# A fused attention, expert and mixing kernel: scores of odd units in other PSUM banks, half of the copies on VectorE, sums over v later

## The chip, the cores and the metric

The kernel runs on one core of one Trainium2 chip. The metric is the device time of one execution in microseconds. Before the change three runs gave 429.08, 429.33 and 431.17 us, median 429.33 us. The engines are TensorE (PE; PEld is its weight load), VectorE (DVE), ScalarE (ACT), GpSimd (POOL), and SyncE (SP), which issues the loads and stores.

## What is computed

Three parts in a row, for batch 2, sequence 768 and width 512. The change concerns the first, an attention of 8 heads with a local window and block summaries:

```
scores_l = q @ k.T / 8, kept where |i - j| < 16
k_sum, v_sum = max of k, mean of v over blocks of 32 tokens
scores_s = q @ k_sum.T / 8 + log(32)
a = softmax(concat(scores_l, scores_s))
attn = a @ concat(v, v_sum)
```

The second routes each token to one of 8 experts (two layers of 512x1024 and 1024x512, relu), the third is a trigonometric token mix with a channel mix behind it.

## The kernel before

**Units.** The attention runs over 24 units k = 3n + g. The pair n (0 to 7) is a batch and two heads, g (0 to 2) is a third of the 768 tokens. A unit has 256 queries for each of two heads, in four groups of 128 (c = 0 to 3). Each group of 64 queries sees a window of 96 keys and 24 block summaries, 120 columns in all.

**Steps of a unit.** `attn_s` (L233) computes the scores, eight matmuls of 64x120 on TensorE into the tile `sps`; units of even and odd k use different columns of the same two PSUM banks. Then VectorE adds the mask, scales and takes each row's minimum, four instructions (L249, called *mins* below), and ScalarE takes the exponential, four instructions (L251, *exps*). `attn_t` (L255) transposes the result in four matmuls on TensorE, and ScalarE copies it out of PSUM into a tile of `ptl` (L259, *copy*). `attn_v` (L261) multiplies with v into the tile `ops`, which has two PSUM banks of its own (pool `psO`). `attn_n` (L273) divides by the sum, on VectorE.

**Keys.** For each pair, `load_k` and `load_q` bring k and q in. `k_windows` (L209) spreads k into overlapping windows, on GpSimd from the second pair on. `k_max` (L220) takes the block maxima on VectorE: of the next pair's first third at g = 0, of its other two thirds at g = 1 (L223). Then GpSimd writes the summaries behind the windows (L229), and the scores of that pair can start.

**Sums over v.** `vsum(b, x)` (L176) sums blocks of v of batch b with matmuls over the third x (L181, *pv*). After the last third ScalarE copies the sums (L183), one matmul spreads them (L186, *pvb*), ScalarE copies the result into the first rows (L194) and GpSimd copies these to the other places in three instructions (L195, then twice L197). The products with v of thirds 0, 1, 2 need the first, second and third of these copies.

**Order.** The loop at L904 fixes the order on every engine: each engine runs its instructions in the order in which the program emits them. An iteration k emits the scores of unit k, the preparation of the next pair's keys, one piece of side work, the transposes and the copy of unit k-1, loads and sums over v, and products with v. Products of the first batch start at k = AV0 = 9 (up to three an iteration until they have caught up), those of the second batch at k = AV1 = 15. The table `VSUM` says in which iteration the sums over v go (first batch at k = 3, 5, 6 and the spreading at 7; second batch at 11, 11, 12 and 13). `SP` loads v of the second batch in iterations 6 and 9. When the first batch's last unit is normalized, at k = 14, the transposes for the router (`gate_T`) and then the routing (`route0`) begin. After the loop the expert weights are split and multiplied, and then the mix runs, all in a fixed order too.

Of the kernel before, what the change touches and what calls it, by code (L numbers as in the profile page):

```python
# [10 lines left out]
F32 = mybir.dt.float32  # L11
# [19 lines left out]
KC = W + NB  # L31
# [59 lines left out]
def tile_attn_moe_mix(ctx: ExitStack, tc: tile.TileContext, qT, kT, vp, gw, w1, w2, wth, wtok, wch, cst, msk, out):  # L91
    nc = tc.nc
    V, A, G, T, SP = nc.vector, nc.scalar, nc.gpsimd, nc.tensor, nc.sync

    def pool(name, bufs, stack=ctx, **kw):
        kw.setdefault("reuse_waits", "tile")
        return stack.enter_context(tc.tile_pool(name=name, bufs=bufs, **kw))
# [55 lines left out]
    psO = pool("psO", 2, sA, space=PSUM)  # L153

    sps = psS.tile([128, 2, 512], F32, name="sps")
# [7 lines left out]
    ptl = {k: pts[k] if k < NPT else spare[:, k - NPT] for k in range(NPT + NSP)}  # L163
# [7 lines left out]
    def load_v(b, g):  # L171
        SP.dma_start(vall[:, vslot(b, g)].rearrange("p c v -> p (c v)"), vp[b, g, :, 0:4 * VW])

    vps = {}

    def vsum(b, x):  # L176
        if x == 0:
            vps[b] = psM.tile([128, DM], F32, name="pv", tag="m")
        for c in range(4):
            rhs = vall[0:W, vslot(b, x), c].rearrange("p (h d) -> p h d", d=D1)[:, :, 0:D]  # L180
            T.matmul(vps[b][32 * c:32 * c + 32, :], ind[0:W, 32 * x:32 * x + 32], rhs, start=x == 0, stop=x == 2)  # L181
        if x == 2:
            A.copy(svt, vps[b])  # L183
            yield
            pb = psM.tile([128, DM], F32, name="pvb", tag="m")
            T.matmul(pb[W:KC, :], ind[:, 96:120], svt, start=True, stop=True)  # L186
            one_w = pb[W:KC, :].rearrange("p (h d) -> p h d", d=D)
            dst = [vall[W:KC, vslot(b, g)].rearrange("p c (h d) -> p c h d", d=D1)[:, :, :, 0:D] for g in range(3)]
            first = dst[0][:, 0]

            def wide(t, n):
                return t.unsqueeze(1).to_broadcast([NB, n, H, D])

            A.copy(first, one_w)  # L194
            G.tensor_copy(dst[0][:, 1:4], wide(first, 3))  # L195
            for g in (1, 2):
                G.tensor_copy(dst[g], wide(first, 4))  # L197

    def load_k(n):
        b, p = divmod(n, NP)  # L200
        kcs[n] = kp.tile([128, 800], F32, name="kc", tag="kc")
        SP.dma_start(kcs[n], kT[b, 2 * p:2 * p + 2, :, 0:800].rearrange("h d s -> (h d) s"))

    def load_q(n):
        b, p = divmod(n, NP)
        qf[n] = qp.tile([128, S], F32, name="qf", tag="qf")
        SP.dma_start(qf[n], qT[b, 2 * p:2 * p + 2].rearrange("h d s -> (h d) s"))

    def k_windows(n, lo=0, hi=NT):  # L209
        kc = kcs[n]  # L210
        if lo == 0:
            ka[n] = kp.tile([128, NT, KC], F32, name="ka", tag="ka")
        win = bass.AP(tensor=kc.tensor, offset=kc.offset + 64 * lo, ap=[list(kc.ap[0]), [64, hi - lo], [1, W]])
        dst = ka[n][:, lo:hi, 0:W]
        if n == 0:
            A.copy(dst, win)
        else:
            G.tensor_copy(dst, win)

    def k_max(n, lo, hi):  # L220
        if lo == 0:
            kss[n] = st.tile([128, NB], F32, name="ks", tag="ks", bufs=2)
        V.tensor_reduce(kss[n].rearrange("p (c x r) -> p x c r", c=4, x=3)[:, lo:hi],  # L223
                        kcs[n][:, 16 + 256 * lo:16 + 256 * hi].rearrange("p (x c r j) -> p x c r j", c=4, r=2, j=32),
                        axis=AX.X, op=ALU.max)
        if hi == 3:
            ks = kss.pop(n)
            for a_, b_ in ((0, 4), (4, NT)) if n == 0 else ((0, NT),):
                (V if n == 0 else G).tensor_copy(ka[n][:, a_:b_, W:KC], ks.unsqueeze(1).to_broadcast([128, b_ - a_, NB]))  # L229
# [1 line left out]
    kss = {}  # L231

    def attn_s(n, g):  # L233
        x = (3 * n + g) % 2
        ps = [[sps[:, h, 240 * x + 120 * a:240 * x + 120 * a + KC] for a in range(2)] for h in range(2)]
        for a in range(2):
            for r in range(2):
                for h in range(2):
                    t = 4 * g + 2 * a + r
                    hs_ = slice(64 * h, 64 * h + 64)  # L240
                    T.matmul(ps[h][a][64 * r:64 * r + 64, :], qf[n][hs_, 64 * t:64 * t + 64], ka[n][hs_, t, :],  # L241
                             start=True, stop=True)
        neg = sp.tile([128, 4, KC], F32, name="neg", tag="neg")
        mn = st.tile([128, 4], F32, name="mn", tag="mn")
        for c in range(4):
            a, h = divmod(c, 2)
            t = 2 * g + a
            v = 0 if t == 0 else (2 if t == NT // 2 - 1 else 1)
            V.tensor_tensor_reduce(out=neg[:, c, :], in0=ps[h][a], in1=mk[:, v, :], scale=-0.125, scalar=3.0e38,  # L249
                                   op0=ALU.add, op1=ALU.min, accum_out=mn[:, c:c + 1])  # L250
            A.activation(neg[:, c, :], neg[:, c, :], AF.Exp, bias=mn[:, c:c + 1], scale=-1.0)  # L251
            micro(1)
        return neg

    def attn_t(k, neg):  # L255
        tps = psT.tile([128, 4, 128], F32, name="tps", tag="t")
        for c in range(4):
            T.transpose(tps[0:KC, c, :], neg[:, c, :], idn)
        A.copy(ptl[k][0:KC], tps[0:KC])  # L259

    def attn_v(k):  # L261
        n, g = units[k]
# [597 lines left out]
    def micro(n=2):  # L860
        for _ in range(n):
            micro1()
# [7 lines left out]
    units = [(n, g) for n in range(B * NP) for g in range(3)]  # L870
    NG = len(units)
    HB = NG // 2
    AV0, AV1 = 9, 15
    VSUM = {3: [(0, 0)], 5: [(0, 1)], 6: [(0, 2)], 11: [(1, 0), (1, 1)], 12: [(1, 2)]}, (7, 13)
    spread = None
    todo, fill, norm = [], [], []
    pend, nsp, LS = None, 0, 3
# [14 lines left out]
    def finish(k, kk, ops):  # L892
        attn_n(kk, ops)
        b_, p_ = divmod(units[kk][0], NP)
        if p_ == NP - 1:
            g_ = units[kk][1]
            store_x(b_, g_)
            fill.append((k, b_, 2 * g_))
            fill.append((k, b_, 2 * g_ + 1))
            if b_ == 0 and g_ == 2:  # L900
                state["bg"] = route0()
                state["tok"], state["cool"] = "hop", 0

    for k in range(NG + 8):  # L904
        state["k"] = k
        for kk, ops in norm:
            finish(k, kk, ops)
        norm = []
        if k == AV0:
            todo.sort(key=lambda x: (units[x][1], x))  # L910
        if k < NG:
            n, g = units[k]
            cur = attn_s(n, g)
            if n + 1 < B * NP:
                if g == 0:
                    k_windows(n + 1)
                    k_max(n + 1, 0, 1)
                elif g == 1:
                    k_max(n + 1, 1, 3)
            if g == 0 and 0 < n < B * NP - 2:  # L920
                load_k(n + 2)
                load_q(n + 2)
        if 13 <= k < 19:
            SP.dma_start(yd[256 * (k - 13):256 * (k - 12), :].rearrange("(p a) (r c) -> p (a r) c", p=128, c=128),
                         zro.unsqueeze(1).to_broadcast([128, 8, 128]))
        if k == 12:
            V.tensor_copy(tri, cs[:, C_TRI:C_TRI + 128])
        side(k, False)
        if AV0 <= k < AV1 and len(todo) > 2 and todo[0] < HB:
            kk = todo.pop(0)  # L930
            finish(k, kk, attn_v(kk))
        if pend is not None:
            attn_t(k - 1, pend)
            todo.append(k - 1)
        pend = cur if k < NG else None
        for x in {6: (0, 1), 9: (2,)}.get(k, ()):
            load_v(1, x)
        if k in VSUM[1]:
            next(spread, None)
        for b_, x in VSUM[0].get(k, ()):  # L940
            spread = vsum(b_, x)
            next(spread, None)
        cnt = 0
        while todo and cnt < 2 and (k >= (AV0 if todo[0] < HB else AV1) and len(todo) > 1 or k >= NG):
            kk = todo.pop(0)
            norm.append((kk, attn_v(kk)))
            cnt += 1
        if k >= NG and nsp < LS and (0, nsp) in raws:
            split_piece(0, nsp)
            nsp += 1  # L950
        if k >= NG and not todo and not norm:
            break
        side(k, True)
# [53 lines left out]
    for n in range(8 * NL + 8):  # L1007
        j, q = divmod(n, 8)
        for half in range(2):
            h = 2 * q + half  # L1010
# [36 lines left out]
    for q in range(8):  # L1047
        n = 8 * NL + 8 + q
# [419 lines left out]
```

## Time and profile before

| | |
|---|---|
| median of 3 runs | 429.33 us |
| profiled execution | 431.33 us, span of its core 429.5 us |
| busy in the span: PE, DVE, ACT, POOL | 404.9, 305.2, 230.9, 106.4 us |
| mean granted TensorE clock | 0.987 of full speed |
| attention units 0 to 9, first to last scores | 5.53 to 24.53 us |
| last product with v | 72.7 us |
| DMA moved | 76.32 MB, mean 178 GB/s |

The profiled execution is 2.0 us above the median of the runs; 1.83 us of its time lie outside the span. Times in the rows below are microseconds from the start of the span. A matmul with fp32 operands shows as two records, so eight matmuls read x16 in a timeline.

### The profile page before, as it was taken

The numbers are of one execution on the slowest core, as the hardware profiler recorded it, in microseconds if no ns is written. First come the engines' busy times: TensorE is split into PE (matmuls) and PEld (weight loads), VectorE is DVE, ScalarE is ACT, GpSimd is POOL, SyncE is SP. The second block draws the span as 40 slices with busy tenths as digits, with TensorE's granted clock in tenths as the row PEclk, the third lists the DMA queues.
The fourth block names the chain that finished last, engine by engine and source line by source line (L and its number), as shares of the span: only waits on it lengthen the run. The fifth ranks groups of instructions, "written<-read, shape, count | busy, mean of one in ns | idle before, by whom it ended". The sixth has DMA issues, their size and how long they took to land. (4 is left out here: it accounts for less than half of the span.)

```text
span 429.5 us, 8298 instructions
## 1 busy us (share of the span) xinstructions
PE 404.9 (94%) x3109; PEld 343.1 (80%) x3109; DVE 305.2 (71%) x733; ACT 230.9 (54%) x423; POOL 106.4 (25%) x95
## 2 busy tenths in 40 slices
PE   7889998799899999999998999999999999999993
PEld 6465766598798989898987878888888788889883
DVE  5476687779797968987899588797988843622731
ACT  5875857346466667775678566564654421211300
POOL 6171703510122105040210121443334710100000
PEclk9999999899899999999999999999999999999997
DMA  8994938773787968988587352322300010100022
GB/s 301 410 389 140 338 113 275 284 277 106 263 271 246 346 225 280 335 276 310 187 300 236 127 216 99 102 75 79 119 24 8 28 39 26 49 14 27 14 75 79
DMA packets 43441, 76.32 MB, mean 178 GB/s; under 512 B 3328, under 2 KB 25088, under 8 KB 42624
## 3 DMA queue, kind: packets, MB, share of 16 engines
q1 hardware_dynamic: 41312, 68.89, 46.8%
q0 software_dynamic: 2080, 6.82, 4.3%
q8 instruction: 26, 0.43, 0.4%
q14 instruction: 23, 0.19, 0.2%
HBM read 62.85 MB, written 12.85 MB: 176 GB/s over the span
## 5 line engine op out<-in xcount | busy, mean ns | idle before, releaser
L596 DVE TENSOR_TENSOR wlo<-wraw,whi 128x1024 fp32r<-128x1024 f32 x53 | 64.4, 1219 | 13.2 <-ACT whi L595 13.2
L595 ACT CAST whi<-wraw 128x1024 fp32r<-128x1024 f32 x56 | 58.1, 1047 | 3.8 <-DMA wraw<-in_w_dram 2.7
L751 POOL DMA_INDIRECT yd<-y,ixs x13 | 16.6, 1274 | 121.8 <-ACT y L711 100.7
L251 ACT ACTIVATE neg<-neg,mn 128x120 f32<-128x120 f32 x96 | 30.3, 385 | 18.6 <-DVE mn L249 18.2
L633 PE MATMUL psh<-xl,whi 128*128 128x256 f32 x192 | 32.3, 291 | 1.9 <-DVE xl L619 1.9
L633 PE MATMUL psh<-xh,whi 128*128 128x256 f32 x192 | 32.5, 293 | 0.6 <-DVE hl L639 0.6
L633 PE MATMUL psh<-xh,wlo 128*128 128x256 f32 x192 | 31.7, 288 | 0.0
L704 PE MATMUL psy<-whi,hh 128*128 128x512 f32 x96 | 30.7, 401 | 0.0
L1203 POOL TENSOR_TENSOR r<-r,x 128x512 f32<-128x512 f32 x10 | 13.1, 1307 | 69.9 <-ACT r L1198 69.9
L704 PE MATMUL psy<-wlo,hh 128*128 128x512 f32 x96 | 29.8, 392 | 0.0
L704 PE MATMUL psy<-whi,hl 128*128 128x512 f32 x96 | 29.8, 392 | 0.0
L633 PEld LDWEIGHTS psh<-xl,whi 128*128 128x128 f32 x192 | 27.5, 198 | 2.4 <-DVE xl L619 2.4
L633 PEld LDWEIGHTS psh<-xh,whi 128*128 128x128 f32 x192 | 27.7, 199 | 1.7 <-DVE hl L639 0.8
L249 DVE CUSTOM_DVE_ANT_0 neg<-sps,mk 128x120 f32<-128x120 f32 x96 | 21.9, 278 | 9.6 <-PE sps L241 6.7
L633 PEld LDWEIGHTS psh<-xh,wlo 128*128 128x128 f32 x192 | 27.4, 198 | 0.0
L772 ACT ACTIVATE dg<-raw 128x768 f32<-128x768 f32 (+1 forms) x20 | 16.4, 818 | 18.7 <-issue 3.7
L1266 DVE SCALAR_TENSOR_TENSOR o<-psch,xTr 128x512 f32<-128x512 f32 (+1 forms) x8 | 4.4, 552 | 28.7 <-PE psch L1260 28.7
L638 ACT ACTIVATE hh<-psh 128x512 fp32r<-128x512 f32 x24 | 14.3, 595 | 17.2 <-PE psh L633 17.1
L639 DVE SCALAR_TENSOR_TENSOR hl<-psh,hh 128x512 fp32r<-128x512 f32 x24 | 16.5, 687 | 8.9 <-ACT hh L638 8.7
L704 PEld LDWEIGHTS psy<-whi,hl 128*128 128x128 f32 x96 | 18.0, 188 | 4.0
L704 PEld LDWEIGHTS psy<-wlo,hh 128*128 128x128 f32 x96 | 18.0, 188 | 3.9
L604 POOL DMA_INDIRECT xg<-xd,ixg x13 | 15.5, 1196 | 22.1 <-DVE ip L413 19.1
(456 smaller groups left out, 1122.9 us busy)
## 6 DMA issues: line engine op xcount, KB each, us to landing
wraw<-in_w_dram SPq DMA_DIRECT2D x56, 512.0 KB, 4.7
raw<-in_wtok_dram SPq DMA_DIRECT2D x12, 768.0 KB, 6.6
vall<-in_v_dram SPq DMA_DIRECT2D x6, 1040.0 KB, 9.7
kc<-in_k_dram SPq DMA_DIRECT2D x8, 400.0 KB, 6.9
qf<-in_q_dram SPq DMA_DIRECT2D x8, 384.0 KB, 7.1
xd<-xs SPq DMA_DIRECT2D x6, 512.0 KB, 5.5
yd<-zro SPq DMA_DIRECT2D x6, 512.0 KB, 6.7
x<-yd SPq DMA_DIRECT2D x12, 256.0 KB, 2.7
```

The lines of the kernel that those rows point to most:

```text
L249: V.tensor_tensor_reduce(out=neg[:, c, :], in0=ps[h][a], in1=mk[:, v, :], scale=-0.125, scalar=3.0e38, op0=ALU.add, op1=ALU.min, accum_out ...
L251: A.activation(neg[:, c, :], neg[:, c, :], AF.Exp, bias=mn[:, c:c + 1], scale=-1.0)
L595: A.copy(hi, r)
L596: (G if j == 0 and q < 3 else V).tensor_tensor(lo, r, hi.bitcast(F32), op=ALU.subtract)
L604: G.indirect_dma_start(out=t, out_offset=None, in_=xd[0:S, :] if j < 2 else xd, in_offset=bass.IndirectOffsetOnAxis(ap=ixg[:, c:c + 1], ax ...
L633: T.matmul(ps[:, mm, :], a[:, c, fs], x[:, c, :], start=n == 0, stop=n == 11)
L638: A.activation(hh, ps, AF.Relu)
L639: V.scalar_tensor_tensor(hl, ps, 0.0, hh.bitcast(F32), op0=ALU.max, op1=ALU.subtract)
L704: T.matmul(ps, a[:, f, ts_], w[:, f, :], start=q == 0 and n == 0, stop=q == 3 and n == 5)
L751: G.indirect_dma_start(out=yd, out_offset=bass.IndirectOffsetOnAxis(ap=ixs[:, c:c + 1], axis=0), in_=ysb[j, r], in_offset=None)
L772: A.activation(g, hw.bitcast(F32), AF.Copy, scale=2.0 ** -112)
L1203: eng[0].tensor_tensor(r, r, x, op=ALU.mult)
```

## The change

Four things change, all in the attention loop. (1) Units of odd k below AV0 put their scores into two tiles of the pool `psO`, the banks that the products with v use later. (2) The copy of transposed units of odd k below AV0 goes to VectorE. (3) AV0 becomes 10. (4) The table of sums over v moves back: the first batch to k = 4, 7, 8 with the spreading at 9, the second to 12, 12, 13 and 14; the spreading is now emitted right behind the scores of its iteration. The loads of v of the second batch stand in iterations 7, 8 and 10.

```diff
+    AV0, AV1 = 10, 15
...
     def attn_s(n, g):
-        x = (3 * n + g) % 2
-        ps = [[sps[:, h, 240 * x + 120 * a:240 * x + 120 * a + KC] for a in range(2)] for h in range(2)]
+        k = 3 * n + g
+        x = k % 2
+        if x and k < AV0:
+            bank = [psO.tile([128, 2, KC], F32, name=f"spo{h}", tag="o") for h in range(2)]
+            ps = [[bank[h][:, a, :] for a in range(2)] for h in range(2)]
+        else:
+            ps = [[sps[:, h, 240 * x + 120 * a:240 * x + 120 * a + KC] for a in range(2)] for h in range(2)]
...
-        A.copy(ptl[k][0:KC], tps[0:KC])
+        if k < AV0 and k % 2:
+            V.tensor_copy(ptl[k][0:KC], tps[0:KC])
+        else:
+            A.copy(ptl[k][0:KC], tps[0:KC])
...
-    AV0, AV1 = 9, 15
-    VSUM = {3: [(0, 0)], 5: [(0, 1)], 6: [(0, 2)], 11: [(1, 0), (1, 1)], 12: [(1, 2)]}, (7, 13)
+    VSUM = {4: [(0, 0)], 7: [(0, 1)], 8: [(0, 2)], 12: [(1, 0), (1, 1)], 13: [(1, 2)]}, (9, 14)
...
             cur = attn_s(n, g)
+            if k in VSUM[1]:
+                next(spread, None)
...
-        for x in {6: (0, 1), 9: (2,)}.get(k, ()):
+        for x in {7: (0,), 8: (1,), 10: (2,)}.get(k, ()):
             load_v(1, x)
-        if k in VSUM[1]:
-            next(spread, None)
```

The order of SP's instructions stays the same up to the fifth load of keys and beyond; the one difference there is that a fill of `yd` with zeros and a store of `xd` change places near k = 13. GpSimd's order doesn't change at all.

VectorE before, from the last mins of unit 6 (tile `sps`) over the maxima of the next pair's first third to the first mins of unit 7:

```order
L249 ISA neg,mn<-sps,mk 128x120
L249 ISA mn 128x1
L223 TENSOR_REDUCE ks<-kc 128x4x2
L249 ISA neg,mn<-sps,mk 128x120
L249 ISA mn 128x1
```

VectorE now, the same place (`spo` is the tile of an odd unit's scores, `pt_150` the place of unit 5 in `ptl`):

```order
L255 ISA neg,mn<-sps,mk 128x120
L255 ISA mn 128x1
L224 TENSOR_REDUCE ks<-kc 128x4x2
L266 COPY pt_150<-tps 120x512
L255 ISA neg,mn<-spo_442,mk 128x120
L255 ISA mn 128x1
L255 ISA neg,mn<-spo_443,mk 128x120
```

The copy of unit 5 stands between the maxima and the mins of unit 7; the copies of units 1, 3, 7 and 9 are placed in the same way.

TensorE before, from the scores of unit 6 to the first products with v (`pt_145` is unit 0, `pt_148` unit 3):

```order
L241 MATMUL sps<-ka,qf 64x120 x8
L258 MATMUL tps<-idn,neg 120x128 x4
L181 MATMUL pv<-vall,ind 32x512 x4
L241 MATMUL sps<-ka,qf 64x120 x8
L258 MATMUL tps<-idn,neg 120x128 x4
L186 MATMUL pvb<-sv,ind 24x512
L241 MATMUL sps<-ka,qf 64x120 x8
L258 MATMUL tps<-idn,neg 120x128 x4
L241 MATMUL sps<-ka,qf 64x120 x8
L269 MATMUL ops<-vall,pt_145 64x65 x8
L258 MATMUL tps<-idn,neg 120x128 x4
```

TensorE now, first from the transposes of unit 6 to the last third of the sums, in front of unit 9's scores:

```order
L264 MATMUL tps<-idn,neg 120x128 x4
L182 MATMUL pv<-vall,ind 32x512 x4
L247 MATMUL sps<-ka,qf 64x120 x8
L264 MATMUL tps<-idn,neg 120x128 x4
L182 MATMUL pv<-vall,ind 32x512 x4
```

and then from the last of unit 9's scores on:

```order
L247 MATMUL spo_506<-ka,qf 64x120
L187 MATMUL pvb<-sv,ind 24x512
L264 MATMUL tps<-idn,neg 120x128 x4
L247 MATMUL sps<-ka,qf 64x120 x8
L278 MATMUL ops<-vall,pt_145 64x65 x8
L264 MATMUL tps<-idn,neg 120x128 x4
L278 MATMUL ops<-vall,pt_148 64x65 x8
```

The second and third pv stand behind the transposes of units 6 and 7, where they stood behind those of units 4 and 5; the pvb stands behind the scores of unit 9, where it stood in front of those of unit 8.

## Rows read from the trace of the kernel before

**Rows 1.** The page, engines' shares of the chain of waits that ended last.
```profile
PE 42%; ACT 3%; DVE 2%; issue 1%; DMA 1%; ACTq 0%
```

**Rows 2.** Stretches: length, busy us (instructions) by engine, granted clock, DMA share, GB/s.
```profile
5.50:17.90 12.40, 8.72 (x135) 4.92 (x134) 7.43 (x52) 9.97 (x29) 3.46 (x5) 1.00 1.03 402
17.90:24.50 6.60, 5.57 (x74) 2.75 (x71) 3.62 (x26) 4.75 (x13) 1.65 (x3) 1.00 1.04 420
24.50:42.50 18.00, 16.91 (x318) 11.39 (x318) 12.53 (x67) 10.59 (x31) 8.08 (x7) 1.00 0.61 234
42.50:73.40 30.90, 27.84 (x473) 20.76 (x470) 23.05 (x147) 22.59 (x60) 10.84 (x11) 1.00 0.75 236
```

**Rows 3.** Timeline of PE, units 2, 6, 7 and 9: start, length, [idle before <-releaser].
```profile
8.93 0.64 PE L241 MATMUL sps<-ka,qf 64*64 64x120 f32 x16 [0.43 <-DVE mn L249]
...
17.89 0.64 PE L241 MATMUL sps<-ka,qf 64*64 64x120 f32 x16
...
19.59 1.07 PE L181 MATMUL pv<-vall,ind 96*32 96x512 f32 x8 [0.48 <-DMA vall<-in_v_dram]
...
21.75 1.04 PE L186 MATMUL pvb<-sv,ind 128*24 128x512 f32 x2
...
23.29 0.65 PE L258 MATMUL tps<-idn,neg 128*120 128x128 f32 x4
24.53 0.64 PE L241 MATMUL sps<-ka,qf 64*64 64x120 f32 x16 [0.59 <-issue]
```

**Rows 4.** Timeline of ACT: exps and two copies in iteration 7.
```profile
21.99 1.25 ACT L251 ACTIVATE neg<-neg,mn 128x120 f32<-128x120 f32 x4 [0.67 <-DVE mn L249]
23.15 0.56 ACT L259 COPY pt<-tps 120x512 f32<-120x512 f32 x1
23.73 0.58 ACT L194 COPY vall<-pvb 24x512 f32<-24x512 f32 x1
```

**Rows 5.** Timeline of DVE: pair 3's maxima, mins of units 7 and 9, a copy.
```profile
21.34 0.42 DVE L223 TENSOR_REDUCE ks<-kc 128x8 f32<-128x256 f32 x1 [1.74 <-DMA kc<-in_k_dram]
21.67 0.27 DVE L249 CUSTOM_DVE_ANT_0 neg<-sps,mk 128x120 f32<-128x120 f32 x1
...
22.48 0.68 DVE L223 TENSOR_REDUCE ks<-kc 128x16 f32<-128x512 f32 x1
...
25.33 0.28 DVE L249 CUSTOM_DVE_ANT_0 neg<-sps,mk 128x120 f32<-128x120 f32 x1 [0.90 <-ACT neg L251]
...
73.85 0.69 DVE L302 COPY xT<-psx 128x512 f32<-128x512 f32 x1 [0.36 <-PE psx L298]
```

**Rows 6.** DMA issues between 9.5 and 9.9 us: KB, median us to landing.
```profile
kc<-in_k_dram SPq DMA_DIRECT2D x1, 400.0 KB, 11.7
```

**Rows 7.** Timeline of POOL: copies of the first batch's sums.
```profile
24.43 1.47 POOL L195 COPY vall<-vall 24x1536 f32<-24x1536 f32 x1 [0.78 <-POOL ka L229]
25.84 3.74 POOL L197 COPY vall<-vall 24x2048 f32<-24x2048 f32 x2
```

**Rows 8.** Timeline of PE: products of units 0 and 7, scores of 14, products of 12 and 13.
```profile
25.95 0.68 PE L269 MATMUL ops<-vall,pt 121*64 121x65 f32 x14 [0.52 <-POOL vall L195]
...
31.23 0.69 PE L269 MATMUL ops<-vall,wraw 121*64 121x65 f32 x16 [0.55 <-DVE ri L277]
...
42.53 0.64 PE L241 MATMUL sps<-ka,qf 64*64 64x120 f32 x16
...
46.61 1.16 PE L269 MATMUL ops<-vall,pt 121*64 121x65 f32 x32
```

**Rows 9.** Timeline of PE around the first fall of its clock.
```profile
83.44 0.30 PE L484 MATMUL psi<-rh,loh 128*128 128x2 f16 x6 [1.64 <-DVE rh L480]
...
84.52 1.05 PE L633 MATMUL psh<-xl,whi 128*128 128x256 f32 x4
...
88.25 0.64 PE L633 MATMUL psh<-xh,whi 128*128 128x256 f32 x4
```

**Rows 10.** One stretch of PE there: length, busy us, granted clock, DMA share, GB/s.
```profile
85.00:86.00 1.00, 1.00 (x6) 0.50 1.07 420
```

## The prediction

> **What bounds the kernel now.** I began with the chain of waits that ended last: it is nearly all TensorE [rows 1], which from the end of the attention on runs its fixed order almost without a gap. A change that touches only the attention is therefore worth the time by which TensorE reaches that later work sooner or later. So I read the attention by stretches [rows 2]. Up to 24.5 us TensorE has gaps (8.72 of 12.40 us busy, then 5.57 of 6.60), and the DMA queues are full all that time (share 1.03 and 1.04). From 24.5 to 42.5 us it is busy for 16.91 of 18.00 us: there its work is the bound. From 42.5 to 73.4 us 27.84 of 30.90.
>
> In the first stretches the timeline of TensorE shows two kinds of wait. Scores wait for the mins of the unit before, which read the same banks (the row at 8.93) [rows 3]; units 0 to 6 so take 17.89 - 5.53 = 12.4 us, 2.06 each. The sums over v wait for v (the row at 19.59) [rows 3]. VectorE shows a third: at 21.34 us the maxima of pair 3's first third wait 1.74 us for its keys [rows 5]. These were issued at 9.54 us and landed 11.7 us later, at 21.24 [rows 6], because the queue was full ahead of them.
>
> **Before unit 7: a gain that ends at a wait.** With odd units in other banks the scores no longer wait for mins, and ScalarE has eight exps and one copy for two units: in iteration 7 the copy starts 1.16 us behind the exps (21.99 to 23.15) and the next instruction 0.58 behind that (23.73) [rows 4], so 2 x 1.16 + 0.58 = 2.9 us, 1.45 a unit. With start-up and transposes between I take 1.5 to 1.6: scores of unit 6 at 5.53 + 6 x 1.55 = 14.8 in place of 17.89, its mins done at about 16.5. Then VectorE's next instruction is the maxima of pair 3. SP issues the same loads in the same order and the queue was full, so I let the keys land at 21.24 as before. VectorE stands from 16.5 to 21.34, and the whole gain of 3 us is gone. The loads of v in other iterations cost and gain nothing, for the same reason.
>
> **From 21.34 to unit 9's scores.** Now what stands behind the maxima on VectorE counts. Copy of unit 5: starts 0.33 later (21.34 to 21.67 [rows 5]), at 21.67; a copy of this size took 0.69 [rows 5], and the next instruction starts some 0.08 before such an end, as the mins do behind the maxima's 0.42: 22.28. Mins of unit 7 take 0.81 (21.67 to 22.48 [rows 5]), exps start 0.32 behind their start (21.67 to 21.99 [rows 4, 5]): 22.6, last end 23.85. Transposes of unit 7 can begin with the first exps, at best at 23.45, at worst at 23.85; I take 23.45. They last 0.65, a pv 1.07 [rows 3], and the next matmul starts some 0.08 before such an end: 0.57 and 1.0. So unit 9's scores start at 25.0. Before it was 24.53: 0.5 us later. Meanwhile TensorE has done unit 8's scores (about 19.5) and nothing else, a gap of 4 us; before, the third pv and the pvb were done by 22.8.
>
> **From there to the products.** The pvb now follows unit 9's scores. Mins of unit 9 start 0.8 behind the scores (24.53 to 25.33 [rows 3, 5]), exps at 26.13, the copy of the pvb stands behind them on ScalarE: 26.13 + 1.16 = 27.3, and ends at 27.9. GpSimd's first copy starts 0.12 later (23.73 + 0.58 to 24.43 [rows 4, 7]), at 28.0, and the product of unit 0 goes on 1.52 behind that start (24.43 to 25.95 [rows 7, 8]): 29.5 in place of 25.95. TensorE has by then done more than before: one unit's scores, one unit's transposes and the pvb (lengths 0.64, 0.65 and 1.04 [rows 3], less the overlaps 0.57 + 0.57 + 0.97 = 2.1 us). From unit 0's product to unit 14's scores took 42.53 - 25.95 = 16.58 us [rows 8]; less 2.1 it is 14.5, and the wait of 0.55 at unit 7's product [rows 8] should mostly go, since the maxima that held VectorE there move away: 13.9 to 14.5. Unit 14's scores start at 43.8 in place of 42.53, 1.3 us late.
>
> **The second batch.** Its pvb now stands behind unit 14's scores, where it stood in front: 0.97 more. It also runs into GpSimd again: mins 44.6, exps 44.9, copy of the pvb 46.1 to 46.7, GpSimd's first copy 46.8, its second 1.41 later (24.43 to 25.84 [rows 7]) for about 1.95, so unit 13's product waits until 50.2. TensorE would be there at 43.8 + 0.97 + (46.61 - 42.53) + 0.6 = 49.45 [rows 8]: 0.7 us. Sum: 1.3 + 0.97 + 0.7 = **3.0 us later**. What follows is the same order with the same loads hung on it, and shifts as a whole. The bounds of this sum are 1.5 (all steps at their short ends) and 4.0.
>
> **The clock.** [...] If the level is low for some of the gap and the first 1.2 to 2.2 us behind it, that costs 0.5 to 1.7 us; I take 1.0, and keep 0 as the other end.
>
> **Sum:** 3.0 + 1.0 = 4.0 us. The profiled execution took 431.33 us, so 435.3 in its terms. It stood 2.0 us above the median of the runs; against that median of 429.33 I predict **433.3 us**.
>
> [...] The row at 8.93 shows scores waiting 0.43 us for mins in the same banks [rows 3]. [...]
>
> **The rivals.** *(1) No fall of the clock.* The stretch from 5.5 to 17.9 us kept the full clock with TensorE busy for only 70% of it [rows 2], and the new gap may be shorter than I think. Then 3.0 us: 432.3, from 430.8 to 433.3.
> *(2) The delay is taken up later.* Between 42.5 and 73.4 us TensorE idles 3.06 us [rows 2], some of it waiting for VectorE. Where these waits end by work that doesn't hang on TensorE, a late TensorE eats them: between 0 and 3 us of the 3 or 4. Against it: the routing on VectorE starts from the last normalized unit, so it shifts too. It would give 429.5 to 431.
> *(3) Faster.* The keys of pair 3 don't hold VectorE, because they land sooner or were late in this one execution. Then units 0 to 9 run at 1.55: unit 9's scores start at about 19.5, 5.0 earlier than before. The steps behind are as above: the same sum with 19.5 in place of 25.0 is 3.0 - 5.5 = -2.5, so 426.8. It decides from a landing that is 3 us earlier, at about 18.2 us, on. For it: waits of TensorE on mins really go. Against it: a share of 1.03 in every stretch, an unchanged order of loads.
>
> **How the numbers follow.** What I forecast has a chance of 0.50, rival 1 0.23, rival 2 0.17, rival 3 0.10. A measurement of this kernel can tell about 0.5% from no change, 2.15 us. Slower by more: 0.50 + 0.23 = 0.73. Within: 0.17. Faster: 0.10. The range leaves out rival 3 and the lower part of rival 2; at the top it takes the upper ends of both terms, 4.0 + 1.7, and a little for gaps further on that fall into another phase of the clock: 429.5 to 435.5. The forecast's own range is 431.5 to 435.5.
>
> **What would show it.** In the trace of the changed kernel: scores of unit 6 near 14.8 us; VectorE waiting 4 to 5 us for pair 3's keys, until about 21.3; a gap of about 4 us on TensorE in front of unit 7's transposes, and a granted clock of 0.50 in the 4 us behind it; unit 9's scores near 25 to 26; the product of unit 0 waiting for GpSimd's first copy until 29.5 to 30.5; the last product with v 3 to 4 us later than at 72.7. It is wrong if VectorE gets these keys before 19 us, or if unit 14's scores start before 42.5.

## The result, and the profile after

| | before | after |
|---|---|---|
| median, us (6 runs each) | 429.20 (427.01 to 431.17) | 434.33 (432.95 to 437.39) |
| profiled execution, its span, us | 431.33, 429.5 | 432.95, 431.1 |
| mean granted clock in it | 0.987 | 0.988 |

The changed kernel is slower: ratio 1.0131, interval 1.0084 to 1.0177, or 5.1 us between the medians. Its profiled execution is the shortest of its six, and that of before was longer than all its runs; so the spans differ by 1.6 us only, and times are compared by the medians, places by the traces.

The chain that ended last, from the page of the kernel after. It is TensorE as in [rows 1], and the kernel still pays for whatever delays the attention:

```profile
PE 41%; DMA 3%; ACT 3%; DVE 2%; issue 1%; SPq 0%; ACTq 0%
```

The stretches of [rows 2] in the kernel after (length; busy us of PE, PEld, DVE, ACT, POOL; granted clock, DMA share, GB/s):

```profile
5.50:17.90 12.40, 11.42 (x162) 6.72 (x162) 9.16 (x62) 9.64 (x31) 3.46 (x5) 1.00 1.00 392
17.90:24.50 6.60, 3.43 (x35) 1.41 (x34) 2.83 (x16) 1.92 (x7) 1.50 (x2) 0.99 1.06 414
24.50:42.50 18.00, 16.70 (x283) 10.26 (x282) 11.86 (x63) 8.89 (x26) 7.83 (x7) 0.91 0.67 247
42.50:73.40 30.90, 27.39 (x455) 19.17 (x455) 22.30 (x145) 20.96 (x57) 8.73 (x8) 1.00 0.61 189
```

TensorE now works more in the first stretch (11.42 us in place of 8.72) and much less in the second (3.43 in place of 5.57). The DMA queues are as full as before in both (share 1.00 and 1.06, against 1.03 and 1.04). The third stretch shows something else that is new: a granted clock of 0.91.

TensorE after, from unit 6's scores to unit 0's product, the places of [rows 3] (start, length, what; in brackets the idle time ahead and what ended it):

```profile
15.27 0.64 PE L247 MATMUL sps<-ka,qf 64*64 64x120 f32 x16
...
19.55 0.64 PE L247 MATMUL sps<-ka,qf 64*64 64x120 f32 x16
23.36 1.18 PE L264 MATMUL tps<-idn,neg 128*120 128x128 f32 x4 [3.17 <-ACT neg L257]
24.47 1.94 PE L182 MATMUL pv<-vall,ind 96*32 96x512 f32 x8
26.34 1.08 PE L247 MATMUL spo<-ka,qf 64*64 64x120 f32 x16
27.35 1.26 PE L187 MATMUL pvb<-sv,ind 128*24 128x512 f32 x2
...
31.39 0.68 PE L278 MATMUL ops<-vall,pt 121*64 121x65 f32 x14 [1.26 <-POOL vall L196]
```

Unit 6's scores start 2.6 us sooner than before. Then, behind unit 8's scores, TensorE stands 3.17 us for unit 7's exps. After that its matmuls are long: the pv lasts 1.94 in place of 1.07 us and unit 9's scores 1.08 in place of 0.64. The clock, microsecond by microsecond (length, PE busy, granted clock, DMA share, GB/s), shows why:

```profile
24.00:25.00 1.00, 1.00 (x6) 0.71 0.97 408
25.00:26.00 1.00, 1.00 (x8) 0.50 1.04 433
26.00:27.00 1.00, 1.00 (x17) 0.50 1.02 417
27.00:28.00 1.00, 1.00 (x12) 0.58 0.95 385
28.00:29.00 1.00, 1.00 (x6) 1.00 1.03 411
```

After the gap 0.50 is granted for about 3.4 us (2 x 0.29 + 2 + 2 x 0.42, an estimate that counts what a slice lacks of 1.00 as time at 0.50), just where the rows show no wait ahead of TensorE's matmuls.

What the exps of unit 7 waited for stands on VectorE (the places of [rows 5]):

```profile
21.67 0.42 DVE L224 TENSOR_REDUCE ks<-kc 128x8 f32<-128x256 f32 x1 [4.69 <-DMA kc<-in_k_dram]
22.00 0.68 DVE L266 COPY pt<-tps 120x512 f32<-120x512 f32 x1
22.60 0.27 DVE L255 CUSTOM_DVE_ANT_0 neg<-spo,mk 128x120 f32<-128x120 f32 x1
```

The maxima of pair 3 wait for its keys for 4.69 us, where they waited 1.74. The gain of units 0 to 6 has become a longer wait for the same transfer, and the copy of unit 5 and the mins of unit 7 are queued behind it.

Later in the attention TensorE after shows unit 14's scores, unit 13's product, unit 16's scores, the index matmul of the routing, the last products with v and the first transposes of the gathered x (the rows that the routing has DMA fetch for the experts):

```profile
45.26 0.64 PE L247 MATMUL sps<-ka,qf 64*64 64x120 f32 x16
...
51.73 0.69 PE L278 MATMUL ops<-vall,pt 121*64 121x65 f32 x16 [0.56 <-POOL vall L198]
...
52.94 0.64 PE L247 MATMUL sps<-ka,qf 64*64 64x120 f32 x16
...
72.30 0.29 PE L463 MATMUL psi<-rh,loh 128*128 128x2 f16 x6 [0.56 <-DVE rh L459]
...
76.93 1.22 PE L278 MATMUL ops<-vall,pt 121*64 121x65 f32 x32
...
80.85 1.15 PE L625 MATMUL psx<-idn,xg 128*128 128x128 f32 x8
```

TensorE before, unit 16's scores and the same later places:

```profile
48.28 0.64 PE L241 MATMUL sps<-ka,qf 64*64 64x120 f32 x16
...
67.66 0.29 PE L454 MATMUL psi<-rh,loh 128*128 128x2 f16 x6 [0.56 <-DVE rh L450]
...
71.57 1.22 PE L269 MATMUL ops<-vall,pt 121*64 121x65 f32 x32
...
76.47 0.30 PE L616 MATMUL psx<-idn,xg 128*128 128x128 f32 x1 [0.90 <-DMA xg<-xd,ixg]
77.33 0.98 PE L616 MATMUL psx<-idn,xg 128*128 128x128 f32 x7 [0.56 <-DMA xg<-xd,ixg]
```

Unit 14 is 2.73 us late against 42.53 [rows 8], unit 16 4.66. Unit 13's product waits 0.56 us for GpSimd, which it didn't before.

Of these 4.66 us only 1.6 are left at the end of this pair of traces. About 1.0 goes by the next index matmul (83.44 [rows 9], 87.06 after): the wait for the gathered x is gone. Another 1.45 goes by the transpose that stands at 89.69 before and at 91.86 after: in the trace before, the clock was at 0.50 from 83.7 to 87.1 us, behind the wait of 1.64 us [rows 9], and in the trace after, it stayed at 1.00 behind a wait of 1.58 us there. So the two spans lie close together in part because the clock fell in one execution and not in the other; the medians are the better measure.

### The profile page after: what moved, and what is told of

It is laid out like the page before. It is cut to its first block, busy times and chain, and to the rows that moved or that the text cites. A ratio compares the mean times of both kernels' runs of the same rounds, so it can differ in the third digit from the quotient of the medians.

```text
span 431.1 us, 8300 instructions
## 1 busy us (share of the span) xinstructions
PE 407.4 (95%) x3109; PEld 342.2 (79%) x3109; DVE 307.5 (71%) x738; ACT 228.6 (53%) x418; POOL 106.2 (25%) x95
## 4 chain that ended last, share of the span: by engine, by line
PE 41%; DMA 3%; ACT 3%; DVE 2%; issue 1%; SPq 0%; ACTq 0%
PE ya L1243 15%; PE yb L1243 8%; PE pth L1181 8%; PE psch L1268 8%; ACT whi L604 1%; PE psxt L1118 1%; DMA wraw<-in_w_dram 1%; DVE wlo L605 1%; DMA x<-yd 1%; DMA yd<-y,ixs 1%; ACT dg L781 0%; DVE hl L648 0%; PE yb L1234 0%; ACT dl L782 0%; ACT hh L647 0%
## 5 line engine op out<-in xcount | busy, mean ns | idle before, releaser
L257 ACT ACTIVATE neg<-neg,mn 128x120 f32<-128x120 f32 x96 | 30.2, 385 | 24.9 <-DVE mn L255 23.5
L264 PE MATMUL tps<-idn,neg 128*120 128x128 f32 x96 | 18.8, 295 | 4.7 <-ACT neg L257 4.7
L255 DVE CUSTOM_DVE_ANT_0 neg<-sps,mk 128x120 f32<-128x120 f32 x76 | 17.2, 277 | 7.2 <-PE sps L247 5.3
L648 DVE SCALAR_TENSOR_TENSOR hl<-psh,hh 128x512 fp32r<-128x512 f32 x24 | 16.5, 687 | 7.6 <-ACT hh L647 7.4
```

The source lines that it names most:

```text
L648: V.scalar_tensor_tensor(hl, ps, 0.0, hh.bitcast(F32), op0=ALU.max, op1=ALU.subtract)
```

## The experiments

Each kernel was timed against the kernel before on the same chip, in five rounds, and profiled once. The kernel before had medians of 429.67, 429.82, 429.79 and 429.85 us in the four batches of runs.

### Which part loses the time

**The change with the sums back where they were.**

```diff
-    VSUM = {4: [(0, 0)], 7: [(0, 1)], 8: [(0, 2)], 12: [(1, 0), (1, 1)], 13: [(1, 2)]}, (9, 14)
+    VSUM = {3: [(0, 0)], 5: [(0, 1)], 6: [(0, 2)], 11: [(1, 0), (1, 1)], 12: [(1, 2)]}, (7, 13)
...
-            if k in VSUM[1]:
-                next(spread, None)
...
+        if k in VSUM[1]:
+            next(spread, None)
```

> The changed kernel with the sums over v and their spreading back in the iterations and places of before (3, 5, 6 and 7; 11, 11, 12 and 13), the other banks, the copies on VectorE and AV0 = 10 kept. My theory: the loss lies in where the sums now stand on TensorE's order, so nearly all of it goes: within 1 us of the kernel before (about 429), no gap of 3 us on TensorE near 20 to 23 us, unit 14's scores near 42.6 us. Rival (banks or copies cost): still 3 us or more above before.

(AV0 = 10 and the loads of the second batch's v stay as in the change.) Measured: 429.48 us, ratio 1.0004 (0.9977 to 1.0031). TensorE of this kernel, the second and third pv and unit 9's scores:

```profile
17.11 1.08 PE L182 MATMUL pv<-vall,ind 96*32 96x512 f32 x8 [1.75 <-DMA vall<-in_v_dram]
...
19.80 1.07 PE L182 MATMUL pv<-vall,ind 96*32 96x512 f32 x8 [0.46 <-DMA vall<-in_v_dram]
...
24.53 0.74 PE L247 MATMUL spo<-ka,qf 64*64 64x120 f32 x16
```

With the sums at their old places, banks, copies and loads cost nothing and bring nothing that stands out of the interval (-1.0 to 1.3 us). With the sums where they were, TensorE itself stands for v, so the scores can't run ahead; unit 9 starts at 24.53, as before [rows 3].

**The sums alone**, with AV0 = 10, old banks and all copies on ScalarE:

```diff
-    AV0, AV1 = 9, 15
-    VSUM = {3: [(0, 0)], 5: [(0, 1)], 6: [(0, 2)], 11: [(1, 0), (1, 1)], 12: [(1, 2)]}, (7, 13)
+    AV0, AV1 = 10, 15
+    VSUM = {4: [(0, 0)], 7: [(0, 1)], 8: [(0, 2)], 12: [(1, 0), (1, 1)], 13: [(1, 2)]}, (9, 14)
```

(with the spreading placed as in the change; the loads of the second batch's v stay in iterations 6 and 9, as before)

> The kernel before with the sums over v, their spreading and AV0 = 10 of the changed kernel alone; scores of all units in the old banks, all copies on ScalarE. My theory: nearly the whole loss comes back, 2.5 to 5 us above before (432 to 434), with a gap of 2 to 3 us on TensorE while the keys of pair 3 are awaited. Rival (banks or copies cost): within 1 us of before.

Measured: 433.19 us, ratio 1.0083 (1.0050 to 1.0116). TensorE, unit 9's scores and unit 0's product:

```profile
25.00 0.64 PE L241 MATMUL sps<-ka,qf 64*64 64x120 f32 x16
...
29.62 0.68 PE L269 MATMUL ops<-vall,pt 121*64 121x65 f32 x14 [0.93 <-POOL vall L195]
```

The sums carry the loss: with them alone 3.5 us are lost, and AV0 = 10 without them costs nothing (the kernel above). One thing in that expectation missed: TensorE has no gap of 2 to 3 us here. From 8 us on its largest is 0.94 us, with scores in the same banks waiting for mins on the way (0.53 us at 19.70, 0.93 at 22.85), and the clock stays at 1.00 from 14 to 31 us (it was at 0.50 from 9.9 to 13.2 us in this execution). VectorE still waits at pair 3's maxima (1.93 us, until 21.57), and unit 9 still comes at 25.00. So unit 9 comes late without the other banks, and without a fall of the clock ahead of it.

**The change with all copies on ScalarE:**

```diff
-        if k < AV0 and k % 2:
-            V.tensor_copy(ptl[k][0:KC], tps[0:KC])
-        else:
-            A.copy(ptl[k][0:KC], tps[0:KC])
+        A.copy(ptl[k][0:KC], tps[0:KC])
```

> The changed kernel with all copies on ScalarE. My theory: the copy of unit 5 behind the maxima delays the chain by 0.6 us at unit 9's scores, but it then waits at GpSimd's first copy anyhow; 0.3 to 0.6 us less than the changed kernel. Rival (the copies on VectorE are the cost): 2 us or more less than the changed kernel.

Measured: 432.42 us, ratio 1.0082 (1.0050 to 1.0113). In its profiled execution (429.44 us, its lowest) the maxima start at 20.60 us, the gap ahead of unit 7's transposes is 1.74 us and there is no fall of the clock behind it (1.00 from 8 to 31 us). Most of the shorter gap is the earlier keys (1.07 us of 1.43). The five copies on VectorE (of 24) aren't the main part of the loss, since it is still there without them. Whether they add to it isn't settled: by the ratios this kernel is 2.1 us under the changed one, more than the 0.3 to 0.6 expected and as much as the rival asked for, but the two were timed on different chips and their intervals overlap.

### What the clock costs

**Filler in the gap**, first 30, then 48 matmuls whose result isn't used:

```diff
+        if k == 8:
+            dummy = psM.tile([128, 128], F32, name="dummy", tag="m")
+            for x in range(48):
+                T.matmul(dummy, one, one, start=x == 0, stop=x == 47)
         if pend is not None:
             attn_t(k - 1, pend)
```

With 30:

> The changed kernel with 30 small bf16 matmuls on a constant tile, whose result nobody reads, in TensorE's gap in front of unit 7's transposes (they should fit into the 3.2 us). It leaves the computation as it is. My theory: the clock isn't lowered behind the gap (granted 1.00 from 23 to 30 us), unit 9's scores start near 25.2 in place of 26.3, and the time falls by 0.7 to 1.5 us against the changed kernel. Rival (the low clock there is hidden by the wait for GpSimd): the clock stays up, but unit 0's product goes on no sooner than 31.4 us and the time is the same.

Measured: 432.69 us, ratio 1.0077 (1.0045 to 1.0109). The filler lasted 1.85 us, 1.18 us of gap stayed, and the clock fell all the same (0.50 from 24.2 to 27.6 us in the profiled execution): the theory missed its places. It didn't decide what the clock costs, either: over its nine runs the time at 0.50, estimated from the mean clock as in the last section, was 8.2 us on average, against 13.7 in the changed kernel, so the clock may have held in others of them. With 48:

> The changed kernel with 48 matmuls of one bf16 tile on itself (30 in the earlier run) ahead of unit 7's transposes; their result is not used, the output stays whole. They fill TensorE's gap of 3.2 us behind unit 8's scores. Theory (the gap makes the clock fall to 0.50 for the next 3.4 us, which costs about 1.3 us there): the filler takes about 3 us, the gap left is under 0.5 us, the granted clock stays at 1.00 from 23 to 30 us, unit 9's scores come at 25.0 to 25.5, time 432 to 433.3 us. Rival (filler of this kind doesn't keep the clock, as in the earlier run): granted 0.50 from about 24 to 27.5 again, unit 9 near 26, time 433 to 435. If the filler is longer than the gap, unit 7's transposes start up to 0.5 us later than without, and unit 9 with them.

Measured: 432.43 us, ratio 1.0057 (1.0035 to 1.0079). TensorE of this kernel:

```profile
19.80 2.85 PE L945 MATMUL dummy<-one 128*128 128x128 bf16 x48
22.99 1.19 PE L264 MATMUL tps<-idn,neg 128*120 128x128 f32 x4 [0.34 <-ACT neg L257]
24.11 1.07 PE L182 MATMUL pv<-vall,ind 96*32 96x512 f32 x8
25.10 0.64 PE L247 MATMUL spo<-ka,qf 64*64 64x120 f32 x16
...
29.71 0.68 PE L278 MATMUL ops<-vall,pt 121*64 121x65 f32 x14 [1.25 <-POOL vall L196]
```

Now the clock is 1.00 from 8 to 31 us, the pv lasts 1.07 us, and unit 9 and unit 0's product come at 25.10 and 29.71. The forecast for a clock that stays at 1.00 was 25.0 and 29.5.

This kernel and the changed one had been timed on different chips, so both were run again **side by side**, the changed kernel first:

> The changed kernel once more, unaltered, beside the one with 48 filler matmuls on the same chip. Its first comparison had six runs of it (434.33 us, ratio 1.0131); the two halves of the change alone came out at 1.0014 (second batch's sums) and 1.0067 (first batch's), whose sum is 0.5 per cent less. Theory (the clock's fall behind the 3 us gap is part of the changed kernel's loss in every run): 433 to 434.5 us, 0.5 to 2 us above the filled kernel, unit 9's scores near 26 us with 0.50 granted ahead of them. Rival (the first six runs lay high; the fall costs nothing on average): 432 to 433 us, the same as the filled kernel.

> The changed kernel with 48 filler matmuls ahead of unit 7's transposes, as before (432.43 us, ratio 1.0057), now on the same chip as the changed kernel itself. Theory: 432 to 433 us, 0.5 to 2 us under the changed kernel, clock at 1.00 from 20 to 30 us, unit 9's scores at 25.0 to 25.5. Rival: the same time as the changed kernel to within 0.5 us.

Measured: the changed kernel 434.57 us (433.19 to 439.0, ratio 1.0137, 1.0084 to 1.0189), the filled one 431.93 (431.48 to 433.21, ratio 1.0062, 1.0036 to 1.0088). That is 2.64 us for the filler, a little over the 0.5 to 2 expected. TensorE of the changed kernel, second execution:

```profile
23.23 1.33 PE L264 MATMUL tps<-idn,neg 128*120 128x128 f32 x4 [2.88 <-ACT neg L257]
24.49 1.94 PE L182 MATMUL pv<-vall,ind 96*32 96x512 f32 x8
26.36 1.08 PE L247 MATMUL spo<-ka,qf 64*64 64x120 f32 x16
27.36 1.90 PE L187 MATMUL pvb<-sv,ind 128*24 128x512 f32 x2
...
31.52 0.68 PE L278 MATMUL ops<-vall,pt 121*64 121x65 f32 x14 [0.39 <-POOL vall L196]
```

and of the filled kernel, second execution:

```profile
24.75 0.64 PE L247 MATMUL spo<-ka,qf 64*64 64x120 f32 x16
...
43.24 0.64 PE L247 MATMUL sps<-ka,qf 64*64 64x120 f32 x16
...
50.92 0.64 PE L247 MATMUL sps<-ka,qf 64*64 64x120 f32 x16
```

In this execution of the changed kernel 0.50 was granted not for 3.4 but for 6.8 us, from 23.4 to 30.2: the pvb took 1.90 us, and the transposes behind it, at 29.20, 1.11. Unit 16 came at 53.16 in the changed kernel and 50.92 in the filled one; the keys landed 0.58 us sooner in the latter (maxima at 21.53 and 20.95), so some 1.7 us of that are left for the clock. Over the runs of this pair, the mean clock gives an estimate of 13.7 us at 0.50 for the changed kernel and 8.4 for the filled one. On a busy TensorE 5.3 us less at 0.50 are worth about 2.6 us (an estimate), as much as the difference of the medians.

### Which batch, and whose wait

**Only the second batch's sums late**, and **only the first batch's**. The tables (the spreading at 7, 13 as before, at 9, 14 as in the change; loads of the second batch's v as in the change, in both, other than the first of the two texts says):

```diff
+    VSUM = {3: [(0, 0)], 5: [(0, 1)], 6: [(0, 2)], 12: [(1, 0), (1, 1)], 13: [(1, 2)]}, (7, 14)
...
+    VSUM = {4: [(0, 0)], 7: [(0, 1)], 8: [(0, 2)], 11: [(1, 0), (1, 1)], 12: [(1, 2)]}, (9, 13)
```

> The changed kernel with the first batch's sums over v and the loads of the second batch's v at the places of the kernel before; only the second batch's sums stay at their later places (units 12 and 13, spread behind unit 14's scores). It shares out the loss between the two batches. Theory (most of the loss comes from the first batch's part; the second batch's costs about 2 us between units 14 and 16, of which the wait for the gathered x takes back 1 to 1.6): unit 9 at 24.5, unit 14 at 42.7, unit 13's product waits 0.5 to 0.6 us for GpSimd, unit 16 at 50.3 to 50.6, a wait for the gathered x of 0 to 0.3 us left of 1.46; time 429.8 to 431 us. Rival (the second batch's part is the larger and nothing is taken back): 431.5 to 433. Rival (it costs nothing, being taken back entire): 429.0 to 429.8.

> The changed kernel with the second batch's sums over v at the places of the kernel before (units 11 and 12, spread at the end of unit 13's iteration); the first batch's stay at their later places. It is the other half of the run in which only the second batch's were late, which was 0.8 us over the kernel before (ratio 1.0014). Theory (the first batch's part is most of the loss, about 2 to 4 us with the clock's fall): unit 9's scores at 25.0 to 26.4 (26.34 in the changed kernel), unit 14's at 43.6 to 45.5, from there to unit 16's 5.6 to 6.2 us (7.68 in the changed kernel), a wait for the gathered x of 0 to 1 us, time 431.5 to 433.5 us. Rival (the two parts only cost together, since the wait for the gathered x takes up what one alone costs): 429.5 to 431 us, with that wait near zero.

Measured: second batch 430.67 us, ratio 1.0014 (0.9984 to 1.0044); first batch 432.18 us, ratio 1.0067 (1.0042 to 1.0092). The scores of units 14 and 16, with the second batch's sums late:

```profile
43.25 0.64 PE L247 MATMUL sps<-ka,qf 64*64 64x120 f32 x16
...
50.92 0.64 PE L247 MATMUL sps<-ka,qf 64*64 64x120 f32 x16
```

and with the first batch's:

```profile
44.81 0.64 PE L247 MATMUL sps<-ka,qf 64*64 64x120 f32 x16
...
50.55 0.64 PE L247 MATMUL sps<-ka,qf 64*64 64x120 f32 x16
```

From unit 14's scores to unit 16's took 7.67 us in the one, 5.74 in the other. So the second batch's new places do delay unit 16 by 1.9 us. In the time 0.85 us of it shows, in an interval from -0.7 to 1.9. By the medians the first batch's part is the larger. The two losses (0.85 and 2.4 us) add up to 3.2, against 5.1 for the whole; with an interval of more than 1 us on either side of each, that difference isn't settled. The first of the two also missed its places: its clock was at 0.50 from 16.5 to 23.3 us, from within a wait of 1.81 us for v on, so that unit 9 started at 26.25.

**Pair 3's keys first.** The loads of the second and third part of v go behind the keys and queries of pair 3, in the full change and in the kernel with only the first batch's sums late:

```diff
-    load_v(0, 1)
-    load_v(0, 2)
...
                 load_q(n + 2)
+                if n == 1:
+                    load_v(0, 1)
+                    load_v(0, 2)
```

> The changed kernel, with the DMAs of the second and third part of v (first batch) issued on SP behind the keys and queries of pair 3 instead of ahead of them. Theory (what cost the time is that the changed order puts VectorE in front of pair 3's keys and that everything behind waits): the keys land about 15 to 16 us, the maxima of pair 3 run without a long wait, the gap ahead of unit 7's transposes (3.17 us in the changed kernel) goes; unit 9's scores at 22 to 23 us (26.34 there), unit 14's at 41 to 42 (45.26), unit 16's at 48.2 to 49.5 (52.94); time 428.5 to 430.5 us, 1 per cent under the changed kernel. Rival (the later places of the sums over v cost by themselves, whatever the keys do): the sums still end late, unit 9 at 24.5 or later, unit 14 at 44 to 45, time 432 to 434. The second batch's sums still stand at their later places, so unit 14 to unit 16 should still take about 7.6 us (5.75 before).

> The same with the DMAs of the second and third part of v (first batch) issued behind the keys and queries of pair 3: the first batch's sums at their later places, with pair 3's keys early, and the second batch's sums as before. Theory (the first batch's part costs only because VectorE stands at pair 3's maxima until the keys land): the maxima at 16 to 17 us without a wait over 0.5 us, unit 9's scores at 22.5 to 24.5 where the clock stays at 1.00 (the earlier run with early keys had it at 0.50 from 19.4 to 29.3 us in its profiled execution, and unit 9 at 25.69), unit 14's at 41.5 to 43, unit 16's at 47.5 to 49, time 428.5 to 430.3 us, 1.5 to 3 us under the run above. Rival (the places of the sums cost by themselves): time within 1 us of the run above. If the wait for the gathered x takes up whatever is gained ahead of it, the time doesn't fall under that of the kernel before (429.3 to 430.3) even if unit 16 comes earlier.

Measured: 430.77 us, ratio 1.0047 (1.0016 to 1.0077), and 430.62 us, ratio 1.0023 (0.9994 to 1.0053). VectorE of the second kernel:

```profile
16.13 0.41 DVE L224 TENSOR_REDUCE ks<-kc 128x8 f32<-128x256 f32 x1
16.46 0.68 DVE L266 COPY pt<-tps 120x512 f32<-120x512 f32 x1
```

and its TensorE at the second pv, which is now what waits:

```profile
19.44 1.07 PE L182 MATMUL pv<-vall,ind 96*32 96x512 f32 x8 [1.57 <-DMA vall<-in_v_dram]
```

The maxima no longer wait. The reordered loads take 3.6 us off the full change by the ratios (1.0131 and 1.0047; the intervals don't overlap, the chips differ). On one chip they take 1.6 us off the kernel with the first batch's sums late (432.18 to 430.62), but the runs of these two overlap widely (430.42 to 434.29 and 427.88 to 433.57), so that difference by itself isn't clear of noise. The rest isn't won: now v is late, TensorE waits 1.57 us for it, and behind that wait the clock was at 0.50 from 21.0 to 27.7 us (in the first of these kernels, at the same pv and from within a wait of 1.35 us, from 19.3 to 29.5). Unit 9 at 23.94 lies in the range expected even so; units 14 and 16 (43.83, 49.58) and the time, by 0.3 us, don't. The first kernel missed its theory's places, and its time by 0.3 us. The rival with units 9 and 14 as late as ever fits its places (25.69, 44.80), but not its time; its profiled execution took 434.71 us, the longest of its twelve and 3.9 above their median.

### Is there a version that beats both

**Banks alone**, on the kernel before, with AV0 = 10 (the loads of the second batch's v stand in iterations 7, 8 and 10, as in the change):

```diff
-    AV0, AV1 = 9, 15
+    AV0, AV1 = 10, 15
...
+        if x and k < AV0:
+            bank = [psO.tile([128, 2, KC], F32, name=f"spo{h}", tag="o") for h in range(2)]
+            ps = [[bank[h][:, a, :] for a in range(2)] for h in range(2)]
```

> The kernel before with the two parts of the change that cost nothing in the runs so far: scores of odd units in the banks of the products with v, and the products held to unit 10 (AV0 = 10) so that these banks are free; the sums over v where they were, all copies by ScalarE. Theory (the banks shorten the time from one unit's scores to the next as soon as nothing else holds VectorE): unit 6's scores near 15 us (17.89), unit 9 still at 24 to 24.6 because pair 3's maxima wait for the keys, unit 14 at 41.7 to 42.6, unit 16 at 47.3 to 48.3 (48.28); time 428 to 429.4 us. Rival (with the keys late the banks give nothing): unit 16 at 48.2 to 48.6, time 429.3 to 430. Slower than 430 would mean that unit 9's product, one unit later, costs something that no theory here has.

Measured: 430.13 us, ratio 0.9994 (0.9967 to 1.0021): the same as before, and above the range of the theory (429.4) and of the rival (430). Unit 6 started at 18.06, not near 15, because the second pv stands ahead of it and waits 1.34 us for v, until 17.07. Unit 16 came at 47.67, 0.6 us sooner; further on TensorE waits for the gathered x until 77.06 and again until 77.75, where it was 76.47 and 77.33 before, and of that lead nothing shows in the time. No kernel that was run is clearly faster than the one before.

## Why the prediction was right

The sign, the mechanism and the range (429.5 to 435.5) held; the forecast of 433.3 us is 1.0 us under the measured median.

**The gain that ends at a wait.** Unit 6 was forecast at 14.8 and came at 15.27; VectorE was to stand from 16.5 to 21.34 and stood for 4.69 us until 21.67. That the wait is a cause and not only beside the loss is borne out by the full change with the keys first, 3.6 us under the change by the ratios; the 1.6 us of the pair on one chip aren't clear of noise. The other banks, which bring unit 6 forward, aren't needed for the loss: the sums alone lose 3.5 us.

**From the keys to unit 9, and on to unit 14.** The sum of 3.0 us was worked out for a clock of 1.00, and the filled kernel is that case (1.00 from 8 to 31 us in both executions). Its two executions have unit 9 at 25.10 and 24.75 (forecast 25.0), unit 0's product at 29.71 and 29.37 (29.5), unit 14 at 43.59 and 43.24 (43.8), and unit 16 late by 2.99 and 2.64 us (forecast 3.0). In time it lost 2.6 and 2.1 us by the medians, which is rival 1's 3.0 less a little.

**The second batch.** Unit 13's product waits 0.56 us for GpSimd (forecast 0.7), and 14 to 16 takes 1.9 us longer (forecast 0.97 + 0.7 = 1.7). The trace agrees; that only 0.85 us of it shows in the medians when it stands alone was not foreseen, though the interval reaches to 1.9.

**The clock.** This is the term that was mis-sized: 1.0 us, with bounds of 0 and 1.7. That the clock would fall behind the gap was right (0.50 from 24.4 to 27.8 us). But the step let the low clock begin in the gap and reach only 1.2 to 2.2 us behind it. No run shows a fall with these places, from which the step takes its 0.5 to 1.7 us, nor the phase of the clock that the range allows for; both were the author's assumptions. What the traces show in their place is a fall of which none lies in the gap: 0.50 began 1.1 us behind the gap's end and covered the pv, the scores and the start of the pvb (1.94 us for the pv in place of 1.07); in the other execution it began 0.2 us behind and lasted 6.8 us. Side by side the filler was worth 2.64 us. With the sum of 3.0 about right in its places, a fall that cost more than 1.0 us is also why unit 9 (26.34, forecast 25 to 26), unit 0's product (31.39, forecast 29.5 to 30.5) and the last products with v (76.93 against 71.57, 5.4 us late, forecast 3 to 4) came later than the signs said; the last of these varied by 0.7 us between the two executions of the change. The gap itself was 3.17 us and not 4; the prediction's own places, 19.5 + 0.64 to 23.45, give 3.3.

**Rival 2**, that the delay is taken up later, doesn't hold between unit 16, which is 4.66 us late, and the index matmul of the routing at 72.30 us, which is 4.64 late. Behind that the wait for the gathered x did take up about 1 us in this pair of traces. **Rival 3** needed the keys by 18.2 us; in the twelve traces with the loads in the old order the maxima started between 20.4 and 21.7.

**The other banks.** Up to unit 9 the waits of scores on mins (0.43 us at 8.93 [rows 3] and 0.54 at 14.66 before) did go: TensorE's timeline shows none there, in the trace after and with banks alone. The time didn't follow, because the next instruction in line waited for a transfer that came no sooner: on VectorE 4.69 us, until 21.67, in the trace after, and on TensorE 1.34 us, until 17.07, with banks alone.

## What to carry to other kernels

In this kernel two engines waited in turn for a full DMA queue (share 1.00 to 1.06 up to 24.5 us), and the stage that was made faster ended at the next transfer (a wait of 4.69 us in place of 1.74). Before such a change, ask which instruction stands at that transfer in each engine's order, and what is queued behind it. Moving the sums over v out of the wait was a loss (3.5 us with the sums alone): TensorE did them later, on the path, and in the full change it had nothing to do for 3.17 us and then did part of them at a granted clock of 0.50. When a forecast has a term for the clock, cost it from where the low clock begins in the traces and what is queued there, for a longer fall as well as a shorter one (here 6.8 and 3.4 us).

## What the runs showed of the hardware

**How long the clock stayed low varied for the same program**: 3.4 us behind a gap of 3.17 us, 6.8 us behind one of 2.88. From 8 to 31 us no slice of 1 us in the fourteen traces shows less than 0.50. If all that the mean granted clock lacks is lost at 0.50, twice that share, times the span, estimates the time at 0.50: 13.7 us on average over twelve runs of the changed kernel, 8.4 over the second twelve of the filled one (9.1 over the first), 9.4 over the kernel before beside it.

**The clock fell behind some short waits and not behind others.** At the second pv 0.50 began in or behind waits of 1.35 and 1.57 us (keys first) and 1.81 (second batch's sums late), and the clock stayed at 1.00 behind waits of 1.34 (banks alone) and 1.75 (sums put back). At the second index matmul it fell behind 1.64 (before), and not behind 1.58 and 1.63 (the two executions of the change). What decides between them, no run here tells.

**A part of the end of the attention varies too.** From the index matmul to the last products took 4.63 us in the first execution of the changed kernel and 3.71 in the second; where it was long, the wait for the gathered x was gone, and where it was short, 0.85 and 0.59 us of it were left. The filled kernel's two executions did the same (4.68 and 3.72), but with the sums put back a long one (4.64) kept 1.13 and 0.59 us of wait, so the length alone doesn't decide. The cause wasn't traced. The wait before, 0.90 and 0.56 us, can by its sum hide up to some 1.5 us of what the attention loses (an estimate), and may be why small shifts there hardly show in the time.
